# Sparse attention and two feed-forward layers on one core: one weight conversion in two shares its sign step with GpSimd, the first block starts on the strided half of x, and two more mask sums move to VectorE

## The chip, the core and the metric

The kernel runs on one core of a Trainium2 chip. The core has a matrix engine (TensorE, PE in the rows) with its weight loads (PEld), a vector engine (VectorE, DVE), an activation engine (ScalarE, ACT), a general engine (GpSimd, POOL) and a queue engine that issues the transfers (SyncE, SP). The metric is device time of one execution in microseconds, lower is better.

## What is computed

The reference runs three stages in a row: attention of 4 batches of 8 heads over 576 positions (heads 0 to 3 see the last 32 keys, heads 4 to 7 every 32nd key), a feed-forward layer with a squared ReLU, and a second one with a rational function.

```python
scores = q @ k.T / sqrt(D);  scores = where(mask, scores, -1e9)
attn = exp(scores - max);  attn = attn / (sum(attn) + 1e-9);  x = attn @ v
h = maximum(x @ w_in, 0);  x1 = (h * h) @ w_out
h = x1 @ w_in2
g = (a0 + a1*h + a2*h**2 + a3*h**3) / (1 + |b0|*|h| + |b1|*h**2 + 1e-6)
out = g @ w_out2
```

There are 2304 tokens, a width of 512 and an inner width of 2048. The weights arrive as 64-bit floats and are turned into 32-bit ones on the chip.

## The kernel before, in words

**Products.** Each float32 operand of a feed-forward product is split into a high part in TensorE's 32-bit format (fp32r) and the rest, so a product is three matmuls: high by high, high by rest, rest by high (`h_unit` L423 for the first product of a layer, `o_unit1` L468 and `o_unit2` L658 for the second).

**Weight conversion** (`to_f32`, L177 to L192, then `split_w`, L200 and L201). A tile of 512 weights of 128 rows arrives as pairs of 32-bit words, `lo` and `hi`, in `wraw`. ScalarE makes the exponent and the upper mantissa (L188, into `w32`). VectorE shifts and masks that (L189, into a PSUM tile `bits`), joins the sign bit of `hi` (L190) and joins the upper bits of `lo` (L191). GpSimd makes the high part `wh` (L200) and the rest `wl` (L201). For layer 0 there are 32 such conversions, two for each of the 16 slices `f` of the inner width: part 0 holds the slice's columns of w_in, part 1 its rows of w_out. They run in the order `wq` (0 and 1 and 2 of part 0, then part 1 of slice 0, part 0 of slice 3, part 1 of slice 1, and so on alternately). Three go ahead of the first block, then two to each unit (`feed_w`, L531).

**Attention in 13 pieces.** A piece has scores (`at_scores`, L277), a softmax (`at_softmax`), transposes (`at_transpose`), values (`at_values`) and the split of its result into the high part `xh` and rest `xl` of x (`at_out`). Pieces are strided (`s`) or local (`l`). The mask is added in one of two ways. For pieces under `MASK_PE` (L236) TensorE multiplies the mask by an identity into the scores' bank first (L295); for later ones VectorE adds it afterwards (L329). The first three pieces (P0 and P1 strided, P2 local) are the head of the program; the other ten are spread over the units by the table `PLAN`, piece 3 over slices 2, 4 and 5 of the first block, piece 4 over 6, 8 and 9, piece 5 over 10, 12 and 13. P0 and P1 give rows 2 and 3 of the first block's x (`xh10`, `xl10` in the order below), P2 rows 0 and 1 (`xh00`, `xl00`).

**The first layer.** Five blocks of tokens of 16 units each. Unit (j, f) makes the slice's h from four rows kk of x, then ScalarE and VectorE make its square and split it into `gh` and `gl`; two units later `o_unit1` adds it to four accumulators. In block 0 two conversions ride in each unit. `fill` (L490) puts matmuls on a constant tile `warm` ahead of some waits; its counts stand in the table `FILL` (L58).

**What sets the order.** Instructions of the head's pieces and of block 0's conversions on ScalarE stand as written (`pin`, `in_order`, `keep_in_program_order`); the rest is placed by the framework's scheduler, and each engine then runs its own list in that order. An engine whose next instruction waits holds everything behind it.

**The end.** The last unit of the second layer makes its result on VectorE, its high part on ScalarE (L644), its rest on GpSimd (L645), and `o_unit2` of that unit closes the program.

Of the kernel before, what the change touches and what calls it, by code (L numbers as in the profile page):

```python
# [9 lines left out]
F32 = mybir.dt.float32  # L10
# [44 lines left out]


W3 = 54
FILL = {'s0': 8, 's1': 1, 't00': 6, 't01': 2, 's2': 2, 't10': 2, 'v1': 4, 't20': 4, 't21': 2, 'h0': 3}  # L58
S_SLOTS = ((0, 6), (17, 5))
QS_W, QKS_W = 11 * W3, 11 * W3 + S  # L60
QKL_W = 2 * 512 + STRIDE
# [60 lines left out]
def moe_kernel(ctx, tc, qs, vs, ql, vl, w1, w2, a, b, masks, eye, out):  # L122
# [51 lines left out]
        if which and block0[0]:  # L174
            tc.keep_in_program_order(ins)

    def to_f32(layer, f, part, raw, place=None):  # L177

        lo, hi = raw[:, :, 0], raw[:, :, 1]
        w = stage.tile([P, DM], I32, tag="w32", bufs=3, name=f"w32_{layer}_{f}_{part}")
        bits, to = w, w
        if layer == 0 and place:
            to = hi
        if layer == 0:
            bits = psum_w.tile([P, DM], I32, tag="bits", name=f"bits{f}_{part}")
        in_order(layer == 0, nc.scalar.activation(w.bitcast(F32), hi.bitcast(F32), AF.Abs, scale=2.0**-112))  # L188
        nc.vector.tensor_scalar(bits, w, 3, 0x7FFFFFFF, ALU.logical_shift_left, ALU.bitwise_and)  # L189
        nc.vector.scalar_tensor_tensor(bits, hi, -0x80000000, bits, ALU.bitwise_and, ALU.bitwise_or)  # L190
        nc.vector.scalar_tensor_tensor(to, lo, 29, bits, ALU.logical_shift_right, ALU.bitwise_or)  # L191
        return to.bitcast(F32)  # L192

# [4 lines left out]
    def split_w(wh, wl, wf):  # L198

        nc.gpsimd.tensor_scalar(wh, wf, 1.0, 0.0, ALU.mult, ALU.add)  # L200
        nc.gpsimd.tensor_tensor(wl, wf, wh.bitcast(F32), ALU.subtract)  # L201
# [31 lines left out]
    ORDER = [("s", 0, 2), ("s", 0, 3), ("l", 0), ("l", 1), ("s", 1, 2), ("s", 1, 3), ("l", 2),  # L233
             ("s", 2, 2), ("s", 2, 3), ("l", 3), ("s", 3, 2), ("s", 3, 3), ("l", 4)]
    pieces = [Piece(n, *x) for n, x in enumerate(ORDER)]
    HEAD, MASK_PE = 3, 6  # L236
    for p in pieces[:HEAD]:
        p.pinned = True
    pieces[0].homes = ("l8", "l9")
# [171 lines left out]

    gt, acc, lows = {}, {}, []

    def h_unit(layer, j, f, ps):
        n = (WIDTHS2 if layer else WIDTHS)[j]
        wh, wl = wt[layer, f]
        if layer and f % FSTEP[j]:
            ps = ps[:, n:]
        for kk in range(KT):
            c = slice(kk * P, (kk + 1) * P)  # L420
            xh, xl = x_rows(layer, j, kk, n)
            for i, (w, x) in enumerate(((wh, xh), (wh, xl), (wl, xh))):
                nc.tensor.matmul(ps[:, :n], w[:, c], x, start=(kk == 0 and i == 0), stop=(kk == KT - 1 and i == 2))  # L423

    def g_tile(tag, name, n, dtype=F32):
        return gpool.tile([P, 512], dtype, tag=tag, name=name, bufs=3)[:, :n]
# [59 lines left out]
    def fill(what, ps):  # L486


        for _ in range(FILL.get(what, 0)):
            tc.keep_in_program_order(nc.tensor.matmul(ps, warm[:, :P], warm, start=True, stop=True, skip_group_check=True))  # L490
# [14 lines left out]
        nc.scalar.activation(co[:, 6:8], co[:, 4:6], AF.Abs)  # L505


    LAG, LATER = 2, 3
    wq = sorted(((f, p) for f in range(NF) for p in range(2)), key=lambda u: (u[0] + LATER * u[1], -u[1]))


# [19 lines left out]
    def feed_w(n):  # L531
        for _ in range(n):
            load_raw(fed[0])
            if fed[0] < len(wq):
                f, part = wq[fed[0]]
                c = slice(part * DM, (part + 1) * DM)
                wh, wl = wt[0, f] if part else w_place(0, f)
                split_w(wh[:, c], wl[:, c], to_f32(0, f, part, raws[fed[0]], homes[fed[0]][0]))
                fed[0] += 1

    phase, under_way[0] = 0, 2_200_000
# [22 lines left out]
    feed_w(1)  # L564
    at_transpose(P2, 0)
    at_transpose(P2, 1)
    at_values(P2)
    at_out(P2)
    phase, under_way[0] = 1, 0
# [70 lines left out]
    def split2(n):  # L640
        if len(open2) > n:
            j, f, rq = open2.pop(0)
            gh, gl = (l2.tile([P, 512], F32R, tag=f"g{c}2", name=f"g{c}1_{j}_{f}", bufs=4) for c in "hl")
            keep(nc.scalar.copy(gh, rq))  # L644
            keep(nc.gpsimd.tensor_tensor(gl, rq, gh.bitcast(F32), ALU.subtract))  # L645
            gt[1, j, f] = gh, gl

    def o_unit2(j, f):
# [73 lines left out]
    for j, f in steps:  # L722
        block0[0] = j == 0
        if (j, f) not in JOINT:
            attend((j, f))
        while lows:
            lows.pop()()
        if j == 0:
            feed_w(2)
        if (j, f) == (3, 0):  # L730
            load_co()
        ps = psum.tile([P, 512], F32, tag="ps", name=f"h0_{j}_{f}")
        if j == 0:
            fill(f"h{f}", ps)
        h_unit(0, j, f, ps)
        last_act = act1(j, f, ps)
        if (j, f) in JOINT:
            attend((j, f))
        elif 0 < j < 4 and f > (1, 1, -1)[j - 1] and (j, f + 1) not in JOINT and n2 < spills[j - 1] + -(-(spills[j] - spills[j - 1]) * (f + 1) // NF):
            with tc.issue_after(last_act):  # L740
                spill_w(n2 // 2, n2 % 2)
            n2 += 1
            if n2 == 2 * NF:
                first.close()
                l2 = ctx.enter_context(tc.tile_pool(name="l2", bufs=2))
        if j == NB - 1 and NF - EARLY > f >= NF - EARLY - KT:
            load_x1(0, f - (NF - EARLY - KT))
        prev.append((j, f))
        if len(prev) > LAG:
            finish(*prev.pop(0))  # L750
        if j == NB - 1 and f >= NF - EARLY:
            unit2(0, f - (NF - EARLY))
# [30 lines left out]
```

## Time and profile before

| | us |
|---|---|
| time before, median of 3 runs (855.86 to 857.38) | 856.35 |
| the profiled execution, its own time | 857.55 |
| its span, first to last instruction | 855.8 |
| TensorE busy in the span | 846.5 |
| VectorE busy | 600.3 |
| GpSimd busy | 523.2 |
| ScalarE busy | 453.6 |

The profiled execution lies 1.20 us above the median of the three runs, and 1.75 us of its time lie outside the span. TensorE is busy for 99% of the span. A busy stretch of TensorE in the rows is a stretch in which matmuls overlap one another, so what a matmul costs is read from the start of one to the start of the next.

### The profile page before, as it was taken

How to read it: one execution, taken by the hardware profiler on the slowest of the kernel's cores; microseconds unless marked ns; L12 is line 12 of the kernel's file. 1: busy time of each engine (PE TensorE's matmuls, PEld its weight loads, DVE VectorE, ACT ScalarE, POOL GpSimd, SP SyncE). 2: the span in 40 equal slices, each digit the busy share in tenths (PEclk: the TensorE clock that was granted, in tenths of full speed). 3: DMA queues.
4: the chain of work that ended last, by engine and by line, in shares of the span. 5: the costliest groups of instructions: out<-in, count | busy, mean ns of one | idle time of the engine just before them, and what ended most of it. 6: DMA issues, size and time to landing. Idle time of an engine off the chain costs nothing.

```text
span 855.8 us, 14872 instructions
## 1 busy us (share of the span) xinstructions
PE 846.5 (99%) x5762; PEld 720.0 (84%) x5762; DVE 600.3 (70%) x688; ACT 453.6 (53%) x821; POOL 523.2 (61%) x468
## 2 busy tenths in 40 slices
PE   7999999999999999999999999999999999999998
PEld 4788889999888888889999888888888888888896
DVE  5899856556556555552127688888888888888885
ACT  3556534333333343333346566676667666766673
POOL 1687754455444465664334687778777777777664
PEclk9999999999999999999999999999999999999999
DMA  9972535555343374565774300010001000100010
GB/s 338 358 246 78 171 122 200 165 178 188 109 148 106 101 242 156 193 197 194 263 256 148 137 24 25 12 62 13 14 12 62 7 7 6 57 1 0 1 51 25
DMA packets 38246, 99.99 MB, mean 117 GB/s; under 512 B 4384, under 2 KB 8224, under 8 KB 38176
## 3 DMA queue, kind: packets, MB, share of 16 engines
q1 hardware_dynamic: 38176, 99.05, 34.3%
q8 instruction: 45, 0.74, 0.3%
q14 instruction: 25, 0.20, 0.1%
HBM read 72.82 MB, written 26.21 MB: 116 GB/s over the span
## 4 chain that ended last, share of the span: by engine, by line
PE 98%; DVE 1%; DMA 0%; ACT 0%; issue 0%; POOL 0%; SPq 0%; ACTq 0%; POOLq 0%
PE h L423 46%; PE acc L468 23%; PE acc L658 23%; PE ps_vl L361 1%; PE ps_sl L300 1%; PE ps_vs L361 1%; PE ps_ss L300 1%; PE ps_tl L352 1%; PE ps_ts L352 1%; DMA cst<-in_masks 0%; DVE sm L330 0%; PE ps_tl L490 0%; DVE sm L341 0%; PE ps_ss L295 0%; PE ps_sl L295 0%; DVE eal L339 0%
## 5 line engine op out<-in xcount | busy, mean ns | idle before, releaser
L423 PE MATMUL h<-xh,wh 128*128 128x512 f32 (+2 forms) x640 | 237.0, 371 | 0.0
L423 PE MATMUL h<-xh,wl 128*128 128x512 f32 (+2 forms) x640 | 235.6, 368 | 0.0
L423 PE MATMUL h<-xl,wh 128*128 128x512 f32 (+2 forms) x640 | 235.6, 368 | 0.0
L629 DVE RECIPROCAL h<-w 128x512 f32<-128x512 f32 x67 | 224.6, 3353 | 0.0
L624 POOL TENSOR_TENSOR p<-p,hs 128x512 f32<-128x512 f32 x67 | 86.9, 1297 | 97.6 <-ACT p L622 97.5
L423 PEld LDWEIGHTS h<-xh,wh 128*128 128x128 f32 x640 | 120.4, 188 | 18.3 <-issue 0.5
L423 PEld LDWEIGHTS h<-xh,wl 128*128 128x128 f32 x640 | 120.3, 188 | 17.7
L423 PEld LDWEIGHTS h<-xl,wh 128*128 128x128 f32 x640 | 120.4, 188 | 17.5
L468 PE MATMUL acc<-gh,wh 128*128 128x512 f32 (+1 forms) x320 | 118.2, 369 | 0.0
L468 PE MATMUL acc<-gh,wl 128*128 128x512 f32 (+1 forms) x320 | 117.7, 368 | 0.0
L468 PE MATMUL acc<-gl,wh 128*128 128x512 f32 (+1 forms) x320 | 117.6, 367 | 0.0
L658 PE MATMUL acc<-wh,gh 128*128 128x512 f32 x288 | 112.2, 389 | 0.0
L658 PE MATMUL acc<-wh,gl 128*128 128x512 f32 x288 | 112.2, 389 | 0.0
L658 PE MATMUL acc<-wl,gh 128*128 128x512 f32 x288 | 112.1, 389 | 0.0
L619 ACT ACTIVATE sq<-h 128x512 f32<-128x512 f32 x72 | 43.0, 597 | 128.3 <-PE h L423 122.0
L446 POOL TENSOR_TENSOR gl<-r,gh 128x512 fp32r<-128x512 f32 (+1 forms) x59 | 69.5, 1178 | 63.6 <-ACT gh L445 58.4
L627 DVE SCALAR_TENSOR_TENSOR p<-p,co,h 128x512 f32<-128x512 f32 x72 | 53.6, 745 | 69.2 <-POOL p L624 69.2
L438 ACT ACTIVATE r<-h 128x512 f32<-128x512 f32 (+1 forms) x75 | 41.8, 558 | 112.7 <-PE h L423 112.7
L442 DVE TENSOR_TENSOR r<-r 128x512 f32<-128x512 f32 (+1 forms) x59 | 43.6, 739 | 76.3 <-ACT r L438 76.2
L645 POOL TENSOR_TENSOR gl<-rq,gh 128x512 fp32r<-128x512 f32 x72 | 93.4, 1298 | 3.2 <-ACT gh L644 3.2
L626 POOL TENSOR_TENSOR w<-w,sq 128x512 f32<-128x512 f32 x66 | 85.5, 1296 | 0.0
L445 ACT CAST gh<-r 128x512 fp32r<-128x512 f32 (+1 forms) x75 | 43.7, 583 | 57.4 <-DVE r L442 56.9
(115 smaller groups left out, 1324.2 us busy)
## 6 DMA issues: line engine op xcount, KB each, us to landing
wraw<-in_w SPq DMA_DIRECT2D x64, 512.0 KB, 4.3
w_scratch<-sph SPq DMA_DIRECT2D x32, 256.0 KB, 3.9
w_scratch<-spl SPq DMA_DIRECT2D x32, 256.0 KB, 3.2
wh<-w_scratch SPq DMA_DIRECT2D x16, 512.0 KB, 3.9
wl<-w_scratch SPq DMA_DIRECT2D x16, 512.0 KB, 5.3
qks<-in_qs SPq DMA_DIRECT2D x8, 585.0 KB, 5.2
out_dram<-osb SPq DMA_DIRECT2D x18, 256.0 KB, 2.4
xraw<-x_scratch SPq DMA_DIRECT2D x16, 256.0 KB, 2.7
```

The costliest lines, as they stand in the source:

```text
L423: nc.tensor.matmul(ps[:, :n], w[:, c], x, start=(kk == 0 and i == 0), stop=(kk == KT - 1 and i == 2))
L442: nc.vector.tensor_tensor(h, h, h, ALU.mult)
L445: last_act = nc.scalar.copy(gh, h).ins
L446: low = lambda: (nc.vector if psum_h or j == 0 else nc.gpsimd).tensor_tensor(gl, h, gh.bitcast(F32), ALU.subtract)
L468: nc.tensor.matmul(acc[j][e][:, : WIDTHS[j]], w[:, c], g, start=(f == 0 and i == 0), stop=(f == NF - 1 and i == 2))
L619: keep(nc.scalar.activation(sq, h, AF.Square))
L624: keep(nc.gpsimd.tensor_tensor(p1, p1, hs, ALU.mult))
L626: keep((nc.vector if last else nc.gpsimd).tensor_tensor(w, w, sq, ALU.add))
L627: keep(nc.vector.scalar_tensor_tensor(p1, p1, a1, h, ALU.add, ALU.mult))
L629: keep(nc.vector.reciprocal(h, w))
L645: keep(nc.gpsimd.tensor_tensor(gl, rq, gh.bitcast(F32), ALU.subtract))
L658: nc.tensor.matmul(p, g[:, cg], w[:, c], start=(f + d + i == 0), stop=(f + d == NF - 1 and i == 2))
```

## The change

Four edits. In `to_f32`, a conversion with an even number in `wq` (16 of 32) lets GpSimd multiply `hi` twice by 2^-126 in place, which leaves zero with `hi`'s sign; VectorE then joins `w32` (shifted) and that in one step, both read from SBUF, in place of L189 and L190. In the first block `h_unit` takes the rows of x in the order `KK` = 2, 3, 0, 1, and the two first rows of unit 0 (six matmuls) are issued, pinned, between the transposes and the values of the third piece; the three filling matmuls `h0` go. `MASK_PE` falls from 6 to 4, so pieces 4 and 5 get their mask from VectorE. The rest `gl` of the last unit is made on VectorE.

```diff
-FILL = {'s0': 8, 's1': 1, 't00': 6, 't01': 2, 's2': 2, 't10': 2, 'v1': 4, 't20': 4, 't21': 2, 'h0': 3}
+FILL = {'s0': 8, 's1': 1, 't00': 6, 't01': 2, 's2': 2, 't10': 2, 'v1': 4, 't20': 4, 't21': 2}
...
-        nc.vector.tensor_scalar(bits, w, 3, 0x7FFFFFFF, ALU.logical_shift_left, ALU.bitwise_and)
-        nc.vector.scalar_tensor_tensor(bits, hi, -0x80000000, bits, ALU.bitwise_and, ALU.bitwise_or)
+        if zero:
+            z = hi.bitcast(F32)
+            nc.gpsimd.tensor_scalar(z, z, 2.0**-126, 2.0**-126, ALU.mult, ALU.mult)
+            nc.vector.scalar_tensor_tensor(bits, w, 3, hi, ALU.logical_shift_left, ALU.bitwise_or)
+        else:
+            nc.vector.tensor_scalar(bits, w, 3, 0x7FFFFFFF, ALU.logical_shift_left, ALU.bitwise_and)
+            nc.vector.scalar_tensor_tensor(bits, hi, -0x80000000, bits, ALU.bitwise_and, ALU.bitwise_or)
...
-    HEAD, MASK_PE = 3, 6
+    HEAD, MASK_PE = 3, 4
...
-    def h_unit(layer, j, f, ps):
+    def h_unit(layer, j, f, ps, ks=None, keep=False):
...
-        for kk in range(KT):
+        order = range(KT) if layer or j else KK
+        for kk in ks or order:
...
-    LAG, LATER = 2, 3
+    LAG, LATER, KK = 2, 3, (2, 3, 0, 1)
...
-                split_w(wh[:, c], wl[:, c], to_f32(0, f, part, raws[fed[0]], homes[fed[0]][0]))
+                split_w(wh[:, c], wl[:, c], to_f32(0, f, part, raws[fed[0]], homes[fed[0]][0], fed[0] % 2 == 0))
...
     at_transpose(P2, 1)
+    begun = []
+    for f in range(1):
+        ps = psum.tile([P, 512], F32, tag="ps", name=f"h0_0_{f}")
+        h_unit(0, 0, f, ps, KK[:2], True)
+        begun.append(ps)
     at_values(P2)
...
-            keep(nc.gpsimd.tensor_tensor(gl, rq, gh.bitcast(F32), ALU.subtract))
+            keep((nc.vector if (j, f) == (NB2 - 1, NF - FSTEP[-1]) else nc.gpsimd).tensor_tensor(gl, rq, gh.bitcast(F32), ALU.subtract))
...
-        ps = psum.tile([P, 512], F32, tag="ps", name=f"h0_{j}_{f}")
-        if j == 0:
-            fill(f"h{f}", ps)
-        h_unit(0, j, f, ps)
+        if j == 0 and f < len(begun):
+            ps = begun[f]
+            h_unit(0, j, f, ps, KK[2:])
+        else:
+            ps = psum.tile([P, 512], F32, tag="ps", name=f"h0_{j}_{f}")
+            h_unit(0, j, f, ps)
```

How the lists of the engines move, at three places. In the names the figures behind the last underline are a buffer's; `h0_0_0` is h of layer 0, block 0, slice 0, and a conversion's tile `wraw0_5_0` is layer 0, slice 5, part 0. The changed kernel's lines lie up to 16 further down, so its L366 is the L361 of before, its L205 and L206 are L200 and L201, its L349 is L344.

TensorE, from the end of the third piece's values into the first block, before (the 128 values of the piece, `ps_vl0`, stand just ahead of these rows, behind its transposes):

```order
L490 MATMUL h0_0_0_567<-warm_87 128x512
L490 LDWEIGHTS warm_87
L490 MATMUL h0_0_0_567<-warm_87 128x512
L423 MATMUL h0_0_0_567<-xh00_0_527,wh0_0_369 128x512
L423 MATMUL h0_0_1_612<-xh00_0_527,wh0_1_433 128x512
L295 LDWEIGHTS cst_76
L295 MATMUL ps_sl1_0_631<-cst_76 128x384
```

Behind the filling matmuls the first ones of units 0 and 1 read row 0 of x, which comes from the third piece.

TensorE at the same place, now: the end of the six matmuls that stand ahead of the values, and the first of the values:

```order
L429 MATMUL h0_0_0_461<-xh10_0_357,wh0_0_369 128x512
L429 MATMUL h0_0_0_461<-xl10_0_358,wh0_0_369 128x512
L429 MATMUL h0_0_0_461<-xh10_0_357,wl0_0_370 128x512
L366 MATMUL ps_vl0_0_468<-eal0_0_314,vl0_0_104 64x32
L366 MATMUL ps_vl0_0_468<-eal0_1_346,vl0_1_106 64x32
```

Six matmuls of unit 0 on the strided rows have moved ahead of the values, the filling ones are gone, and the first matmuls behind the values read rows 2 and 3 as well, for unit 1.

GpSimd in the head, before: the last step of P1's softmax, the two of P2's (`eal0`), and the first two conversions' split:

```order
L344 TENSOR_TENSOR eas0_3_1_228<-eas0_3_1_228,sm3_82 128x6x54
L344 TENSOR_TENSOR eal0_0_314<-eal0_0_314,sm0_79 128x512
L344 TENSOR_TENSOR eal0_1_346<-eal0_1_346,sm1_80 128x512
L200 TENSOR_SCALAR wh0_0_369<-wraw0_0_0_108 128x512
L201 TENSOR_TENSOR wl0_0_370<-wraw0_0_0_108,wh0_0_369 128x512
L200 TENSOR_SCALAR wh0_1_433<-wraw0_1_0_110 128x512
L201 TENSOR_TENSOR wl0_1_434<-wraw0_1_0_110,wh0_1_433 128x512
```

GpSimd in the head, now:

```order
L349 TENSOR_TENSOR eas0_3_1_228<-eas0_3_1_228,sm3_82 128x6x54
L191 TENSOR_SCALAR wraw0_0_0_108<-wraw0_0_0_108 128x512
L349 TENSOR_TENSOR eal0_0_314<-eal0_0_314,sm0_79 128x512
L349 TENSOR_TENSOR eal0_1_346<-eal0_1_346,sm1_80 128x512
L191 TENSOR_SCALAR wraw0_2_0_112<-wraw0_2_0_112 128x512
L205 TENSOR_SCALAR wh0_0_369<-wraw0_0_0_108 128x512
L206 TENSOR_TENSOR wl0_0_370<-wraw0_0_0_108,wh0_0_369 128x512
L191 TENSOR_SCALAR wraw0_3_0_116<-wraw0_3_0_116 128x512
L205 TENSOR_SCALAR wh0_1_433<-wraw0_1_0_110 128x512
L206 TENSOR_TENSOR wl0_1_434<-wraw0_1_0_110,wh0_1_433 128x512
```

A signed zero (the L191 rows) stands ahead of P2's softmax step, one ahead of slice 0's split, and one, that of slice 3, ahead of slice 1's split.

GpSimd around the softmax of piece 3 (`el1`), before:

```order
L200 TENSOR_SCALAR wh0_4_602<-wraw0_4_0_120 128x512
L201 TENSOR_TENSOR wl0_4_603<-wraw0_4_0_120,wh0_4_602 128x512
L344 TENSOR_TENSOR el1_0_684<-el1_0_684,sm2_81 128x384
L344 TENSOR_TENSOR el1_1_692<-el1_1_692,sm3_82 128x384
L200 TENSOR_SCALAR wh0_2_535<-wraw0_2_1_122 128x512
L201 TENSOR_TENSOR wl0_2_536<-wraw0_2_1_122,wh0_2_535 128x512
```

GpSimd around the softmax of piece 3, now:

```order
L205 TENSOR_SCALAR wh0_4_599<-wraw0_4_0_120 128x512
L206 TENSOR_TENSOR wl0_4_600<-wraw0_4_0_120,wh0_4_599 128x512
L349 TENSOR_TENSOR el1_0_681<-el1_0_681,sm2_81 128x384
L191 TENSOR_SCALAR wraw0_5_0_431<-wraw0_5_0_431 128x512
L349 TENSOR_TENSOR el1_1_689<-el1_1_689,sm3_82 128x384
L191 TENSOR_SCALAR wraw0_6_0_552<-wraw0_6_0_552 128x512
L205 TENSOR_SCALAR wh0_2_542<-wraw0_2_1_122 128x512
L206 TENSOR_TENSOR wl0_2_543<-wraw0_2_1_122,wh0_2_542 128x512
```

One signed zero stands between the piece's two steps, a second one between them and the split of slice 2's part 1.

## Rows read from the trace of the kernel before

**Rows 1.** Stretches: us; busy of PE, PEld, DVE, ACT, POOL; PEclk; DMA share, GB/s

```profile
20.00:23.20 3.20, 1.98 (x47) 1.43 (x48) 2.90 (x11) 2.58 (x8) 1.46 (x2) 0.99 1.02 389
23.20:26.60 3.40, 3.40 (x14) 2.07 (x11) 2.92 (x8) 1.62 (x5) 2.35 (x3) 0.51 0.96 310
...
40.00:130.00 90.00, 90.00 (x787) 74.06 (x786) 76.03 (x137) 48.54 (x92) 63.28 (x65) 1.00 0.48 160
```

**Rows 2.** Waits of TensorE: line, waited for: us in total, times, longest us

```profile
PE ps_vl L361 <- ACT eal L354: 0.5, 1, 0.5
```

**Rows 3.** Timeline of TensorE, head to unit 2: start us, us, what, [idle before <-releaser]

```profile
26.60 0.30 PE L361 MATMUL ps_vl<-eal,vl 64*64 64x32 f32 x2
27.40 2.06 PE L361 MATMUL ps_vl<-eal,vl 64*64 64x32 f32 x126 [0.50 <-ACT eal L354]
29.39 0.82 PE L490 MATMUL h<-warm 128*128 128x512 bf16 x3
...
37.29 0.50 PE L423 MATMUL h<-xh,wh 128*128 128x512 f32 x1
```

**Rows 4.** Timeline of TensorE: transposes and sums of slice 2, then scores with and without mask matmuls

```profile
48.32 0.82 PE L352 MATMUL ps_tl<-ident,el 128*128 128x128 f32 x6
...
51.71 0.39 PE L468 MATMUL acc<-gh,wh 128*128 128x512 f32 x1
...
61.18 0.39 PE L468 MATMUL acc<-gl,wh 128*128 128x512 f32 x1
61.41 0.39 PE L468 MATMUL acc<-gh,wl 128*128 128x512 f32 x1
...
62.02 0.92 PE L300 MATMUL ps_ss<-qks 64*64 64x54 f32 x48
...
126.94 0.39 PE L468 MATMUL acc<-gh,wl 128*128 128x512 f32 x1
127.26 1.48 PE L300 MATMUL ps_sl<-qkl 64*32 64x64 f32 x128
```

**Rows 5.** VectorE from 0 to 125 us by line: busy us, mean ns | idle before

```profile
L190 DVE SCALAR_TENSOR_TENSOR bits<-wraw,bits 128x512 int32<-128x512 int32 x32 | 22.2, 692 | 0.8
L189 DVE TENSOR_SCALAR bits<-w 128x512 int32<-128x512 int32 x32 | 22.1, 690 | 3.7 <-ACT w L188 2.7
...
L446 DVE TENSOR_TENSOR gl<-r,gh 128x512 fp32r<-128x512 f32 x16 | 13.2, 826 | 2.7 <-ACT gh L445 2.6
```

**Rows 6.** GpSimd from 0 to 125 us by line: busy us, mean ns | idle before

```profile
L201 POOL TENSOR_TENSOR wl<-wraw,wh 128x512 fp32r<-128x512 f32 x25 | 34.0, 1361 | 2.1
L200 POOL TENSOR_SCALAR wh<-wraw 128x512 fp32r<-128x512 f32 x25 | 18.0, 720 | 13.9 <-DVE wraw L191 12.1 <-DVE sm L342 1.1 <-issue 0.2
```

**Rows 7.** Line L446: durations ns min/median/max, first and last start us

```profile
L446 DVE TENSOR_TENSOR gl<-r,gh x16: 678/688/1271, 35.8 to 121.7; 128x512 fp32r<-128x512 f32 x16
```

**Rows 8.** Timeline of GpSimd: head, then the steps of piece 3's softmax

```profile
21.74 2.04 POOL L344 TENSOR_TENSOR eal<-eal,sm 128x512 f32<-128x512 f32 x2 [5.77 <-DVE xl L385]
...
25.48 1.29 POOL L201 TENSOR_TENSOR wl<-wraw,wh 128x512 fp32r<-128x512 f32 x1
...
28.08 1.30 POOL L201 TENSOR_TENSOR wl<-wraw,wh 128x512 fp32r<-128x512 f32 x1
...
45.65 2.14 POOL L344 TENSOR_TENSOR el<-el,sm 128x384 f32<-128x384 f32 x2
...
48.56 1.73 POOL L201 TENSOR_TENSOR wl<-wraw,wh 128x512 fp32r<-128x512 f32 x1
```

**Rows 9.** Timeline of ScalarE in the head: the conversion of slice 3

```profile
27.24 0.69 ACT L188 ACTIVATE w<-wraw 128x512 f32<-128x512 f32 x1
```

**Rows 10.** The last rest and the matmuls around it

```profile
848.17 1.29 POOL L645 TENSOR_TENSOR gl<-rq,gh 128x512 fp32r<-128x512 f32 x1 [3.24 <-ACT gh L644]
849.18 0.39 PE L658 MATMUL acc<-wl,gh 128*128 128x512 f32 x1
849.51 0.50 PE L658 MATMUL acc<-wh,gl 128*128 128x512 f32 x1
```

More of the change, by code (lines that the diff above doesn't have):

```diff
@@ L175, in in_order, with to_f32 @@
             tc.keep_in_program_order(ins)
-    def to_f32(layer, f, part, raw, place=None):
+    def to_f32(layer, f, part, raw, place=None, zero=False):
         lo, hi = raw[:, :, 0], raw[:, :, 1]
@@ L422, in h_unit @@
             for i, (w, x) in enumerate(((wh, xh), (wh, xl), (wl, xh))):
-                nc.tensor.matmul(ps[:, :n], w[:, c], x, start=(kk == 0 and i == 0), stop=(kk == KT - 1 and i == 2))
+                ins = nc.tensor.matmul(
+                    ps[:, :n], w[:, c], x, start=(kk == order[0] and i == 0), stop=(kk == order[-1] and i == 2))
+                if keep:
+                    tc.keep_in_program_order(ins)
     def g_tile(tag, name, n, dtype=F32):
```

## The prediction

> **What bounds the kernel now.** I read four views, in this order. The table of busy times first: TensorE is busy for 846.5 of 855.8 us, so the time can only fall by taking matmuls away or by filling the 9 us in which it is idle. The waits of TensorE next: the list has seven entries, none of them later than 28 us of the span, and the longest single one is 1.9 us long or less; the one that this change can reach is 0.50 us ahead of the third piece's values, which wait for ScalarE's copy of the transposed weights [rows 2]. Third, the stretches: TensorE's granted clock is 0.51 from 23.20 to 26.60 us (the lower level, 1.2 GHz), after a stretch in which it was busy for 1.98 of 3.20 us, and 1.00 from 40 to 130 us, where it is busy without a break [rows 1]. There VectorE is busy for 76.03 and GpSimd for 63.28 of 90 us: neither holds TensorE up, so a cheaper conversion is worth nothing by itself. It is worth something if TensorE is made earlier and the weights have to follow. Last, the timeline of the head and of block 0, for what stands between the matmuls.
>
> **Part 1, the head.** The third piece's values cost 2.06 us and follow an idle of 0.50 us; behind them come three filling matmuls, 29.39 to 30.21, so 0.82 us [rows 3]. The change puts six matmuls of unit 0 ahead of the values. They were to be done anyway, so they cost nothing new, and they take longer (six steps of 0.23 us from start to start, as 61.18 to 61.41 [rows 4], make 1.4 us) than the 0.50 us that they cover. They need the first rest `wl`, which is done at 25.48 + 1.29 = 26.77 us [rows 8], and are to start when the transposes end at 26.60; its matmul is the third, so it is wanted at about 27.1. Taken away: 0.50 idle and 0.82 filling. The fill covered the time until x of the third piece is there (ScalarE's copies, then VectorE's rests); now unit 1's six matmuls on rows 2 and 3 and what unit 0 has ready lie there, 1.4 us and more, the same cover. Added: two more switches between long matmuls and the short ones of attention. Such a switch takes 0.32 us from start to start, 126.94 to 127.26 [rows 4], instead of 0.23, so about 0.1 each, 0.20. Net gain 1.12 us; 0.6 if x comes 0.5 late, 1.3 if the switches cost nothing.
>
> One new wait here. On GpSimd the signed zero of slice 3 stands ahead of slice 1's split. It waits for ScalarE's step of slice 3, which ends at 27.24 + 0.69 = 27.93 us [rows 9]. Zero (0.72), `wh` (0.72) and `wl` (1.36) of rows 6 put slice 1's rest at about 30.7 us; before it was there at 28.08 + 1.30 = 29.38 [rows 8]. TensorE wants it about 30.8: values end near 30.2, two matmuls, then this one. I take 0.1 us, bounds 0 and 0.5.
>
> **Part 2, the mask sums.** With the mask matmuls the last long matmul starts at 61.41 and the scores at 62.02, 0.61 us; without them it is 126.94 to 127.26, 0.32 us [rows 4]. So 0.29 us for each of two pieces, 0.58 in all, bounds 0.4 and 0.6. VectorE gets four sums of 324 columns; each is shorter than a conversion's step of 512 columns, 0.69 us [rows 5]. They lie ahead of the pieces' softmax, and their transposes come two units later, 11 us of matmuls; I cost them at nothing. If that cover were gone they would be worth at most 2.8 us.
>
> **Part 3, the conversions.** In 16 of 32, VectorE loses L189 (0.690) and L190 (0.692) and gets one step, 0.55 us or so less to do each time; GpSimd gets one in-place step on 512 columns, like L200, 0.72 us [rows 5, 6], 11.5 us in all. I take 0.72 although the new step writes every second word, which no row shows; bounds 0.65 and 1.1. The new VectorE step reads both inputs from SBUF. The one step in block 0 that does so is L446: 0.678 at best, 1.271 at worst, 0.826 on average [rows 5, 7], against 0.692 with one input from PSUM. So VectorE saves 1.382 - 0.826 = 0.56 us each time, 8.9 us in all, and spends up to 2.8 on the sums.
>
> The Trainium skill speaks against this step. "SBUF — State Buffer", section "SBUF: two separate sides", says that GpSimd and a VectorE step with two SBUF inputs lock one pair of ports for a whole instruction and the other waits it out. The spread of rows 7 agrees in kind; on average the wait there is 0.13 us. If each new step waited as long as the worst, it would save 0.1 instead of 0.56 us.
>
> Does TensorE have to wait for the slower GpSimd? The narrowest place is piece 3. GpSimd's two softmax steps run 45.65 to 47.79; the transposes start at 48.32, and the second half of them, 0.3 later, needs the second step: 0.8 us of room [rows 4, 8]. Then the rest of slice 2's second part ends at 48.56 + 1.73 = 50.29, and its sums start at 51.71, 1.4 us [rows 4, 8]. TensorE will be there some 1.1 us earlier. Ahead of the second softmax step GpSimd has five zeros more, 3.6 us, and it had 13.9 us of idle ahead of L200 in block 0, nearly all of it waiting for VectorE, which is now ahead by four times 0.56 us. What VectorE itself waits for (ScalarE's `gh` of slice 0) does not move, so I reckon that this piece's two steps end 0.7 to 1.1 us earlier than before. New wait there: 0.1 us, bounds 0 and 1.2. Behind it TensorE's reserve only grows, since GpSimd's idle is larger than what is added.
>
> **Part 4, the end.** TensorE's step to the third last unit's matmul is 849.18 to 849.51, 0.33 instead of 0.23, because GpSimd's rest ends at 849.46 [rows 10]. On VectorE it would take 0.69 [rows 7] instead of 1.29 and end 0.6 earlier: gain 0.10, no more, since TensorE has the matmuls ahead of it to do first.
>
> **Sum.** 0.50 + 0.82 - 0.20 + 0.58 + 0.10 - 0.20 = 1.60 us. Against the profiled execution it gives 857.55 - 1.60 = 855.95, span 854.2. That execution lies 1.20 above the median, and the gain has nothing to do with that difference: 856.35 - 1.60 = **854.75**, say 854.7.
>
> **Rivals.**
> (A) Forecast: gain of 1.0 to 2.0 us, 854.3 to 855.4. For it: all of it is work or idle that the chain of TensorE holds.
> (B) GpSimd is late in block 0. The new steps lock each other out as at L446's worst, 1.271 against 0.678, VectorE keeps no lead, and at the two narrow places TensorE waits 0.5 to 1.2 us. That leaves 0 to 1.0 of gain, 855.4 to 856.3. For it: 0.8 us of room and 1.1 us of new lead. By the rule of the Trainium skill on the shared ports, named above, this is the case to come. Against it: GpSimd's 13.9 us of idle.
> (C) Slower. The same wait at piece 3's transposes grows past about 1.2 us, and TensorE's clock falls behind it. The rows show such a case: busy for 1.98 of 3.20 us, then 0.51 for 3.40 us [rows 1], which costs half of that, 1.7 us. With a wait of 1.6 us: 856.35 - 1.60 + 1.6 + 1.7 = 858.05. It decides at a wait of about 1.2 us. Against it: the reckoning above finds 0.1, and in the head a wait of 0.50 us left the clock at 1.00.
> (D) More: neither new wait nor the two switches show, and a hitch in unit 0 goes. From the fill's end at 30.21 to unit 2 at 37.29 are 7.08 us [rows 3]; 24 matmuls of 0.23, 96 of the 128 scores' 1.48 and the mask, 0.29 [rows 4] make 6.9, so 0.2 are left that may come from x's being wanted first: 1.6 + 0.4 + 0.2 = 2.2 us, 854.15.
> That the change does not do what it says is ruled out for the masks and the fill, which are gone from TensorE's list; for the conversion it is B.
>
> **How the numbers follow.** A 0.53, B 0.22, C 0.10, D 0.15. The three runs shown reach from 0.5 below to 1.0 above their median, so about 0.2% (1.7 us) is what a measurement can tell from no change, and the forecast lies right at it. Faster by more, below 854.64: all of D and half of A, 0.42. Slower by more, above 858.06: most of C, 0.08. Within: 0.50. The range leaves out C and the tail of D, and takes in what three runs may be off: 853.6 to 856.6.
>
> **What would show it.** TensorE should have no idle between the third piece's transposes and unit 2, which should start near 36.1 instead of 37.29; six matmuls on `xh` should stand ahead of the values. The sums of slices 3 and 7 should be followed by scores after about 0.32 us. The waits of TensorE should lose the line for the values; a new line for GpSimd's `el` or `wl` says B, and a stretch of granted clock near 0.5 behind 40 us says C. VectorE's busy time should fall by some 7 us and GpSimd's grow by some 11. The forecast is wrong if x of the third piece comes late enough to open an idle behind the values, or if a zero takes well over 0.72 us.

## The result and the profile after

The changed kernel takes 861.24 us (median of 19 runs), the kernel before, run beside it, 856.01 us (19 runs). The ratio is 1.0062, with a 95% interval of 1.0042 to 1.0081: slower by 0.6%, some 5.2 us. The forecast was 854.7 us with a range up to 856.6. It was wrong, and in direction too. The ratios here go by all runs but those set aside as slow (here one of the 19, at 2174.79 us), so they need not be the quotients of the two medians.

Executions of one kernel spread over 2.5 to 11 us here, in part because TensorE's granted clock falls in the head in some executions and not in others (the profile of before has 0.51 from 23.20 to 26.60 us [rows 1], the profile of after 1.00 all through the head). So beside the ratio I give the fastest run, and the length of **block 0**, from unit 2's first matmul to the first scores behind the block: before it is 37.29 to 127.26, 89.97 us [rows 3, 4]. It comes from the one profiled execution of each kernel.

The profiled execution of after takes 859.81 us, span 858.0. First the granted clock and busy time by stretches, in the columns of [rows 1]:

```profile
23.20:26.60 3.40, 2.24 (x30) 1.34 (x34) 3.10 (x6) 1.06 (x2) 3.15 (x4) 1.00 0.95 293
34.00:130.00 96.00, 91.49 (x702) 73.73 (x692) 84.40 (x129) 50.09 (x96) 78.13 (x80) 1.00 0.51 175
```

Behind unit 2 TensorE is busy for 91.49 of 96 us, where before it had no break [rows 1]. Its waits from 18 to 132 us, where the kernel before had none for `h`:

```profile
PE h L429 <- POOL wl L206: 1.8, 2, 1.2
PE h L429 <- DVE es L344: 1.8, 1, 1.8
...
PE h L429 <- ACT r L447: 0.8, 1, 0.8
PE h L429 <- POOL wh L205: 0.7, 1, 0.7
PE ps_ss L305 <- issue: 0.7, 1, 0.7
```

The wait for the third piece's values is gone, as forecast. In its place units of `h` wait for GpSimd's splits, for VectorE and for ScalarE, and scores once for something that the profile doesn't name ("issue"). TensorE's timeline, from the first transposes of the third piece on, shows where in the head, and where block 0 begins and ends:

```profile
21.54 0.60 PE L357 MATMUL ps_tl<-ident,eal 128*128 128x128 f32 x4
...
23.71 0.50 PE L429 MATMUL h<-xh,wh 128*128 128x512 f32 x1 [0.70 <-POOL wh L205]
25.09 0.50 PE L429 MATMUL h<-xh,wl 128*128 128x512 f32 x1 [0.65 <-POOL wl L206]
...
34.04 0.50 PE L429 MATMUL h<-xh,wh 128*128 128x512 f32 x1
...
129.72 0.70 PE L305 MATMUL ps_sl<-qkl 64*32 64x64 f32 x47
```

Two things are to be seen. The early matmuls wait 0.70 us for slice 0's `wh` and 0.65 for its `wl`, more than the 0.50 they were to cover. And block 0 is 129.72 - 34.04 = 95.68 us long, 5.7 more than before, though 0.58 us of mask matmuls were taken out. VectorE and GpSimd up to 128 us, by line as in [rows 5, 6]:

```profile
L455 DVE TENSOR_TENSOR gl<-r,gh 128x512 fp32r<-128x512 f32 x16 | 19.9, 1243 | 2.1 <-ACT gh L454 2.1
L192 DVE SCALAR_TENSOR_TENSOR bits<-w,wraw 128x512 int32<-128x512 int32 x16 | 17.2, 1077 | 4.4 <-POOL wraw L191 3.7
...
L195 DVE SCALAR_TENSOR_TENSOR bits<-wraw,bits 128x512 int32<-128x512 int32 x16 | 11.1, 694 | 0.4
L194 DVE TENSOR_SCALAR bits<-w 128x512 int32<-128x512 int32 x16 | 11.0, 687 | 1.7 <-ACT w L188 1.1
...
L205 POOL TENSOR_SCALAR wh<-wraw 128x512 fp32r<-128x512 f32 x25 | 21.0, 839 | 3.5 <-DVE wraw L196 3.0
L191 POOL TENSOR_SCALAR wraw<-wraw 128x512 f32<-128x512 f32 x16 | 12.8, 797 | 3.3 <-ACT w L188 2.2
```

The new step L192 takes 1.08 us on average and not 0.83, the rests `gl` 1.24 and not the 0.826 of [rows 5], and VectorE waits 3.7 us for the zero. Idle ahead of these steps was 3.7 + 0.8 = 4.5 us [rows 5] and is now 4.4 + 1.7 + 0.4 = 6.5. Added up: 17.2 us for L192, 2.0 more idle and 19.9 - 13.2 = 6.7 more for `gl` make 25.9, against 16 times 1.382 = 22.1 us of removed steps. So the new step itself saved 4.9 us, about half of what was forecast, and the rests and the idle took 8.7: VectorE saved nothing, these lines took 3.8 us more. GpSimd's idle ahead of `wh` fell from 13.9 [rows 6] to 3.5 us.

One place shows how that reaches TensorE. Rows of VectorE, GpSimd and TensorE between 61 and 68 us:

```profile
62.25 0.70 DVE L192 SCALAR_TENSOR_TENSOR bits<-w,wraw 128x512 int32<-128x512 int32 x1 [1.06 <-POOL wraw L191]
...
63.59 1.82 DVE L455 TENSOR_TENSOR gl<-r,gh 128x512 fp32r<-128x512 f32 x1
...
66.94 0.88 DVE L344 TENSOR_TENSOR es<-ps_ss,sm 128x324 f32<-128x324 f32 x2
```

```profile
61.58 0.64 POOL L191 TENSOR_SCALAR wraw<-wraw 128x512 f32<-128x512 f32 x1
62.30 1.17 POOL L205 TENSOR_SCALAR wh<-wraw 128x512 fp32r<-128x512 f32 x1
63.55 1.31 POOL L206 TENSOR_TENSOR wl<-wraw,wh 128x512 fp32r<-128x512 f32 x1
64.83 1.08 POOL L205 TENSOR_SCALAR wh<-wraw 128x512 fp32r<-128x512 f32 x1
```

```profile
67.57 0.47 PE L429 MATMUL h<-xh,wh 128*128 128x512 f32 x1 [1.79 <-DVE es L344]
```

VectorE stands 1.06 us for the zero. Then its rest begins 0.04 us behind a split of GpSimd's and takes 1.82 us: it ends 0.55 us after that split. That is no single case: of the 32 VectorE steps with two SBUF inputs up to 128 us (16 of L192, 16 rests), 22 began while a GpSimd step was running, and all 22 ended 0.54 to 0.56 us behind the end of that step; the other ten took 0.68 to 0.70 us. In this profile the price of such a step is thus what is left of the step that it meets. The two halves of the wait here, 1.06 and 1.82 - 0.69 = 1.13 make 2.2 us by which the softmax's steps behind them on VectorE come late. They read scores out of PSUM, the next unit of `h` needs the bank, and TensorE waits 1.79 us.

At the tail the forecast holds: the matmuls of the last unit follow one another every 0.23 us, without the 0.33 of [rows 10]. VectorE's rest takes 0.69 us (GpSimd's took 1.29) and TensorE has no wait there.

### The profile page after: what moved, and what is told of

Read it like the earlier page. It is cut to its first block, busy times and chain, and to the rows that moved or that the text cites. A ratio compares the mean times of both kernels' runs of the same rounds, so it can differ in the third digit from the quotient of the medians.

```text
span 858.0 us, 14841 instructions
## 1 busy us (share of the span) xinstructions
PE 843.2 (98%) x5751; PEld 717.6 (84%) x5755; DVE 605.9 (71%) x677; ACT 452.9 (53%) x821; POOL 539.9 (63%) x483
## 4 chain that ended last, share of the span: by engine, by line
PE 87%; DVE 5%; DMA 4%; POOL 2%; ACT 1%; issue 1%; SPq 1%; DVEq 0%; POOLq 0%
PE h L429 42%; PE acc L672 23%; PE acc L477 20%; DMA wraw<-in_w 3%; DMA vl<-in_vl 1%; DVE gl L455 1%; DVE bits L192 1%; DVE wraw L196 1%; POOL wl L206 1%; PE ps_vl L366 1%; SPq L149 1%; POOL wh L205 1%; DVE bits L195 0%; PE ps_sl L305 0%; POOL wraw L191 0%
```

## The experiments

Of the kernels whose text says that signs or values are joined wrongly or left out, the outputs are not the reference's; the instructions are as described.

### Each part alone

The theories: the ports (**P**: VectorE's steps with two SBUF inputs and GpSimd's steps hold each other up), the masks (**M**), and the head (**H**: its lead is merely eaten).

**Zeros alone.** The kernel before with this in `to_f32`, for every even conversion:

```
+            z = hi.bitcast(F32)
+            nc.gpsimd.tensor_scalar(z, z, 2.0**-126, 2.0**-126, ALU.mult, ALU.mult)
+            nc.vector.scalar_tensor_tensor(bits, w, 3, hi, ALU.logical_shift_left, ALU.bitwise_or)
```

> The kernel before with the signed zero on GpSimd in every second conversion, and nothing else. Theory P (the ports: VectorE's new step and its rests both read two SBUF inputs and are held up by GpSimd's steps, and hold those up): the new step about 1.0 to 1.1 us on average, the rests L446 about 1.2 instead of 0.83, GpSimd's high parts 0.83 instead of 0.72, VectorE's busy time in block 0 not lower, TensorE waits for weights or for the softmax in block 0: 2 to 4 us slower, ratio 1.002 to 1.005. Theory M (the two mask sums hold the scores' banks, the zero is harmless by itself): 0.998 to 1.001. Theory H (the head's new order makes TensorE early and the waits only eat that lead): 1.000.

Measured: 862.45 us against 855.95, ratio 1.0069 (1.0044 to 1.0095); block 0 is 96.44 us long. The zeros alone bring the whole loss, so M and H fall as its cause. P's steps came near what was expected (0.96, 1.17 and 0.84 us), its price did not: the loss lies above P's 1.002 to 1.005.

```profile
L451 DVE TENSOR_TENSOR gl<-r,gh 128x512 fp32r<-128x512 f32 x16 | 18.7, 1167 | 4.9 <-ACT gh L450 4.7
L192 DVE SCALAR_TENSOR_TENSOR bits<-w,wraw 128x512 int32<-128x512 int32 x16 | 15.3, 959 | 8.0 <-POOL wraw L191 7.4
L205 POOL TENSOR_SCALAR wh<-wraw 128x512 fp32r<-128x512 f32 x25 | 20.9, 838 | 3.6 <-DVE wraw L196 3.1
```

The longest wait of TensorE in block 0 is 2.65 us. ScalarE's, GpSimd's, VectorE's and TensorE's rows there, and the stretches behind it (columns of [rows 1]):

```profile
107.86 0.66 ACT L188 ACTIVATE w<-wraw 128x512 f32<-128x512 f32 x1 [1.89 <-POOL wl L206]
108.43 0.58 ACT L443 ACTIVATE r<-h 128x512 f32<-128x512 f32 x1
```

```profile
103.54 0.66 POOL L191 TENSOR_SCALAR wraw<-wraw 128x512 f32<-128x512 f32 x1 [0.91 <-ACT w L188]
105.16 1.00 POOL L205 TENSOR_SCALAR wh<-w 128x512 fp32r<-128x512 f32 x1 [0.97 <-DVE w L196]
106.24 1.59 POOL L206 TENSOR_TENSOR wl<-w,wh 128x512 fp32r<-128x512 f32 x1
```

```profile
105.00 0.68 DVE L451 TENSOR_TENSOR gl<-r,gh 128x512 fp32r<-128x512 f32 x1
105.60 1.11 DVE L192 SCALAR_TENSOR_TENSOR bits<-w,wraw 128x512 int32<-128x512 int32 x1
```

```profile
109.15 0.47 PE L428 MATMUL h<-xh,wh 128*128 128x512 f32 x1 [2.65 <-ACT r L443]
```

```profile
106.50:109.15 2.65, 0.00 (x0) 0.03 (x1) 2.44 (x5) 1.25 (x3) 1.87 (x2) 1.00 0.47 176
...
110.65:114.06 3.41, 3.41 (x10) 2.64 (x9) 3.41 (x7) 0.99 (x4) 3.33 (x3) 0.50 0.03 10
```

Read from TensorE backwards: it waits for ScalarE's `r`, which stands in ScalarE's queue behind a conversion's first step, which waits for a buffer that GpSimd's rest sets free at 107.83. GpSimd's `wh` began beside VectorE's `gl` and took 1.00 where it takes 0.72 [rows 6]; its `wl` began beside L192 and took 1.59 where 1.29 is the least in this stretch; ahead of them GpSimd stood 0.91 us for ScalarE and 0.97 for VectorE. TensorE works again from 109.15, at first at a granted clock of 1.00; from 110.65 the clock is 0.50 (the lower of its two levels) for 3.41 us, which costs half of that, 1.7 us.

**Masks alone.**

```
-    HEAD, MASK_PE = 3, 6
+    HEAD, MASK_PE = 3, 4
```

> The kernel before with the mask of pieces 4 and 5 summed on VectorE, and nothing else. Theory P: 0.6 us of mask matmuls gone, VectorE in time: 0.999 to 1.000. Theory M: a wait of TensorE for VectorE's subtract of pieces 4 and 5 (h of slices 7 and 11) of 0.5 to 2 us each, 1.001 to 1.004.

Measured: 855.78 us, ratio 0.9990 (0.9965 to 1.0015), the fastest run 853.89 against 854.31. In the profile block 0 takes 89.38 us, 0.59 less than before, with no wait in it. M falls, for the masks by themselves. This profile has the clock at 1.00 all through the head and the head's old order, so it is the yardstick for the head of after. Its rows of TensorE, to set beside [rows 3] and the rows of after:

```profile
21.93 0.66 PE L352 MATMUL ps_tl<-ident,eal 128*128 128x128 f32 x4
...
24.31 2.06 PE L361 MATMUL ps_vl<-eal,vl 64*64 64x32 f32 x126 [0.50 <-ACT eal L354]
...
34.22 0.50 PE L423 MATMUL h<-xh,wh 128*128 128x512 f32 x1
```

Unit 2 starts at 34.22 with the old head at full clock and at 34.04 with the new one. That is no gain of the new order, since the third piece's transposes, up to which nothing of TensorE's work has changed, begin 0.39 us earlier in the profile of after (21.54 against 21.93). From there to unit 2 are 12.29 us in the old order and 12.50 in the new one; where 1.12 us were forecast, nothing was gained.

**Head alone** (`KK`, `begun`, no fill).

> The kernel before with the first block on rows 2, 3, 0, 1 of x, six matmuls of unit 0 ahead of the third piece's values and no fill h0; no zero, no mask sums, the last rest on GpSimd. Theories P and M: TensorE's lead of 1.1 to 1.4 us at unit 2 holds in part, 0.998 to 0.9995. Theory H (the lead is eaten by weights that come no earlier): 1.000 with new waits at piece 3's transposes and slice 2's sums, or slower.

Measured: 855.84 us, ratio 1.0005 (0.9974 to 1.0036), the fastest run 855.40, 1.1 above that of before. The waits of TensorE:

```profile
PE h L429 <- POOL wl L206: 0.7, 1, 0.7
PE ps_sl L305 <- issue: 0.6, 1, 0.6
PE h L429 <- POOL wh L205: 0.3, 1, 0.3
```

So without any zero, too, the early matmuls wait for slice 0's `wh` and `wl`. From the transposes to unit 2 are 13.02 us, 0.57 of them a wait for which the profile names no releaser. Block 0 is 90.57, 0.6 longer than before. H's ratio came, but its waits at piece 3's transposes and slice 2's sums did not; and the interval takes in what P and M expected as well.

**All but the zeros.**

> The changed kernel without the signed zero: head, mask sums and last rest stay. Theory P: the loss is gone, ratio 0.997 to 0.999. Theory M: the wait for VectorE's subtract stays, 1.001 to 1.004. A mixture (both parts needed): near 1.000.

Measured: 856.11 us, ratio 0.9983 (0.9958 to 1.0009), the fastest run 855.17. The early matmuls wait 0.3 and 0.6 us for `wh` and `wl`, and later an `acc` waits 0.8 for VectorE's `gl`. From the transposes to unit 2 are 12.25 us, so here too the new order gains nothing. Block 0 is 91.66, 2.3 longer than with the masks alone. H would explain it, what is started earlier waits later, but these are two single profiles, and the time does not show a loss.

### What in the zero costs

Three theories: P as above; the queues (**Q**: ScalarE, GpSimd and VectorE stand for one another, each in its order); the load (**L**: 11 us more for GpSimd). Each kernel is the one with the zeros alone, with one thing changed (two in the last).

**One SBUF input.** The chain stays, the second input goes:

```
-            nc.vector.scalar_tensor_tensor(bits, w, 3, hi, ALU.logical_shift_left, ALU.bitwise_or)
+            nc.vector.tensor_scalar(bits, hi, 3, 0x7FFFFFFF, ALU.logical_shift_left, ALU.bitwise_and)
```

> The zeros alone (conversions of every second piece), but VectorE's step after the zero reads only the zero's tile from SBUF and not the value beside it: its place in the queues, GpSimd's added step and the waits ScalarE to GpSimd to VectorE stay, only the second SBUF input goes (the value without its sign's bits is left out, so the output is not the reference's). Theory P (VectorE's steps with two SBUF inputs and GpSimd's steps hold each other up): the step falls from the 0.96 us mean of the zeros alone to 0.70, gl falls from 1.20 to at most 0.95, and the time to 856 to 858 us. Theory Q (the queues: GpSimd stands behind ScalarE, VectorE behind GpSimd, and each in its order): nothing changes in the waits, 861 to 863 us, idle ahead of the zeros still near 9 us in sum. Theory L (GpSimd simply has 11 us more to do in block 0): 861 to 863 as well.

Measured: 855.87 us against 855.65, ratio 1.0005 (0.9972 to 1.0038). Block 0 is 89.98 long, and TensorE waits nowhere in it. The rows from 20 to 130 us:

```profile
L205 POOL TENSOR_SCALAR wh<-wraw 128x512 fp32r<-128x512 f32 x25 | 19.9, 798 | 2.4 <-DVE wraw L196 1.6
L451 DVE TENSOR_TENSOR gl<-r,gh 128x512 fp32r<-128x512 f32 x16 | 16.6, 1035 | 4.4 <-ACT gh L450 4.2
L192 DVE TENSOR_SCALAR bits<-wraw 128x512 int32<-128x512 int32 x16 | 11.1, 691 | 6.6 <-POOL wraw L191 5.9
```

VectorE still waits 5.9 us for the zeros and GpSimd still has them, so Q and L by themselves fall. The step with one input took 0.68 to 0.70 us each of the 16 times, though 12 of them began while a GpSimd step was running. P's number for the time was almost right, but not that for the rests: `gl` takes 1.035, above the 0.95 expected, and nothing comes of it. GpSimd's idle ahead of `wh` is 2.4 us here, less than in after (3.5), and yet TensorE loses nothing. Nor is it another order of the steps: up to 130 us the lists of VectorE, GpSimd and ScalarE in these two kernels differ by a few neighbouring steps, one in the head and the others around piece 3's softmax, and not around the 2.65 us wait.

**Two SBUF inputs, no zero.** VectorE's joined step stands in place of its two old ones, and GpSimd does nothing more.

> VectorE's step with two SBUF inputs in place of the two old ones in every second piece, and nothing on GpSimd (sign and value are joined wrongly, so the output is not the reference's). Theory P: the step still meets GpSimd's splits, mean 0.80 to 0.95 us, gl 0.85 to 1.0, time 855.5 to 857.5 us. Theories Q and L: VectorE has 16 steps of 0.69 us fewer and nothing new to wait for, 855.3 to 856 us, step near 0.70 to 0.83.

Measured: 855.36 us, ratio 1.0014 (0.9982 to 1.0045), block 0 89.98. The step takes 0.93 us on average and GpSimd's `wh` 0.93, and `gl` 1.03, above the 1.0 that P allowed, and still no loss is to be seen: the slower step by itself doesn't cost either.

**The zero's size on a scratch tile, two SBUF inputs** (nobody waits for GpSimd's step):

```
-            nc.gpsimd.tensor_scalar(z, z, 2.0**-126, 2.0**-126, ALU.mult, ALU.mult)
+            nc.gpsimd.tensor_scalar(zz, hi.bitcast(F32), 1.0, 1.0, ALU.mult, ALU.mult)
```

> As the zeros alone, but GpSimd's added step of 512 columns reads the raw words and writes a tile that nobody reads (sign and value are joined wrongly, so the output is not the reference's): GpSimd has the same steps more, VectorE the same step with two SBUF inputs, but no one waits for the added step, and it does not wait for ScalarE. Theory P: step and gl are as long as with the zeros alone (0.96 and 1.2 us), time 860 to 862.5 us. Theory Q: the time falls to 855.5 to 857 us. Theory L: 860 to 863 us, GpSimd's splits late.

Measured: 858.25 us, ratio 1.0028 (0.9999 to 1.0057), the fastest run 856.18; block 0 is 91.30, with one wait of 1.3 us for ScalarE's `r`. That lies between P and Q. The fastest run, 2.0 us above that of before (854.20), and block 0 point to load and two inputs together costing something, and to the chain adding to it; shown it is not, since the interval takes in no change. The profiled execution is the slowest of the twelve, with the clock at 0.50 in the head up to 36 us, so its block 0 is a weak witness.

**The scratch step, VectorE's old steps.**

> The kernel before with the 16 added GpSimd steps of 512 columns into a tile that nobody reads, and VectorE's three steps as before: GpSimd's load alone. Theory P: gl rises a little above 0.83 us (more GpSimd work beside it), 856 to 857.5 us. Theory Q: 855.8 to 856.5 us. Theory L: 860 to 863 us, TensorE's waits for wh and wl as with the zeros.

Measured: 856.38 us, ratio 1.0000 (0.9969 to 1.0032), block 0 90.49. L falls.

### Where in block 0, and with the masks

**Zeros in the first eight or the last eight even conversions** (the second kernel has `fed[0] >= 16`):

```
-                split_w(wh[:, c], wl[:, c], to_f32(0, f, part, raws[fed[0]], homes[fed[0]][0], fed[0] % 2 == 0))
+                split_w(wh[:, c], wl[:, c], to_f32(0, f, part, raws[fed[0]], homes[fed[0]][0], fed[0] % 2 == 0 and fed[0] < 16))
```

> The zeros alone, but only in the 8 even conversions of the first 16 (whose words are loaded into idle weight buffers and wait there). With the 16 zeros block 0's profile lost 6.5 us, 1.8 of them before the 96 us mark and 4.7 behind it. Theory E (each zero costs its share, half of the zeros half of the loss): 859 us. Theory R (the loss comes where the words go through buffers that must first be set free, in the second 16): 855.7 to 857 us. Theory B (a backlog that is built up early and paid later): near 860 us.

> The zeros alone, but only in the 8 even conversions of the second 16 (whose words are loaded into buffers that earlier conversions must first set free). Theory E: 859 us. Theory R: 860 to 862 us, with TensorE's wait of some 2.7 us for ScalarE's r near the 106 us mark. Theory B: 856 to 858 us, since VectorE and GpSimd come to the second half without arrears.

Measured: 857.86 us, ratio 1.0041 (1.0014 to 1.0069), for the first half (its profile, of an execution of 1412.92 us, gives no block 0); 857.61, ratio 1.0020 (0.9997 to 1.0043), for the second, with block 0 at 91.34 and one wait of 1.3 us for `r`. Together 0.61%, near the 0.69% of all. R falls, since it left the first half without a loss. E comes nearest, though both times lie over 1 us below its 859; B had the second half right (856 to 858) and the first (near 860) not. So the loss is hardly a matter of the second half alone, but the intervals are too wide to say that every zero costs its share.

**The changed kernel with `MASK_PE` at 6.**

> The changed kernel with the mask sums of pieces 4 and 5 on TensorE as before (0.58 us more on TensorE, two long steps of 0.42 us fewer on VectorE in each of these pieces). If the mask sums on VectorE make the zeros' arrears worse (TensorE's wait of 1.8 us for VectorE's subtraction in piece 4): 859 to 860 us. If the two have nothing to do with each other: 861.8 us, the changed kernel's 861.2 and 0.58.

Measured: 862.50 us, ratio 1.0085 (1.0056 to 1.0115), block 0 97.35. The mask sums on VectorE are not shown to make it worse; the wait for VectorE's subtraction shrinks from 1.8 to 0.9 us, and the wait for `r` is back at 2.7.

**Masks, order and tail without the early matmuls and the zeros**, the version that might have beaten both.

> The kernel before with the two mask sums on VectorE, the order 2, 3, 0, 1 in the first slice's units without the six early matmuls and without the last fill, and the tail's last rest on VectorE; no zeros. If the early matmuls were what pulled the waits for slice 0's weights forward and the order itself is worth its 0.5 us of idle time: 854.5 us (masks 0.58, head 0.8 or so). If the head's lead goes whatever the order, since GpSimd's splits of slice 0 come when they come: 855.3 us (masks alone). A loss above 856.5 us speaks against both.

Measured: 857.41 us, ratio 1.0007 (0.9986 to 1.0027), the fastest run 854.58 against 854.08. No gain, and the median lies above the 856.5 that was to speak against both expectations. Its profiled execution lost 3.0 us in the head to a wait for which the profile names no releaser, so its head can't be judged by it. No version here is shown to beat the kernel before; all but the zeros (0.9983) and the masks alone (0.9990, with the lowest fastest run of the changed kernels) come nearest.

### Plain length without the shared lock

What stayed open was which engine's lengthening costs. These three have VectorE's step with one SBUF input, as in the run with one SBUF input, and a plain step more on VectorE, on GpSimd, or on both:

```
+            nc.vector.tensor_scalar(bits[:, :256], bits[:, :256], 0, 0x7FFFFFFF, ALU.logical_shift_left, ALU.bitwise_and)
+            nc.gpsimd.tensor_scalar(z[:, :128], z[:, :128], 2.0**-126, 2.0**-126, ALU.mult, ALU.mult)
```

> As the run in which VectorE's step after the zero reads one SBUF input (855.9 us), but that step is followed by one of 256 columns that reads and writes only PSUM (some 0.4 us): VectorE's conversion is now as long as with two SBUF inputs beside GpSimd, and no lock is held for it. (The value without its sign's bits is left out of the output, as there.) If VectorE's longer step is what costs (the conversions come late, whoever lengthens them): 858 to 862 us. If it is that GpSimd's splits are held up too, or that the two engines are locked into step: 855.5 to 856.5 us.

> As the run with one SBUF input (855.9 us), but GpSimd's zero is followed by one more step of 128 columns on it, 0.2 to 0.3 us, which is what its two splits took longer per zero when VectorE read two inputs (0.84 and 1.42 us where the run with one input has 0.80 and 1.33, twice per zero). If GpSimd's lengthening is what costs: 858 to 861 us. If VectorE's: 855.5 to 856.5 us.

> Both lengthenings at once. If the loss is the sum of what the two engines lose to each other, whatever the reason for it, this comes near the zeros alone: 860 to 862.5 us, with TensorE's wait for ScalarE's r in block 0. If it takes the lock itself (steps that meet at the moment when one waits for the other): 856 to 857.5 us.

Measured (before: 855.66 us, fastest 853.84):

| kernel | median | fastest | ratio, 95% | block 0 |
|---|---|---|---|---|
| VectorE + 0.43 us | 856.31 | 855.05 | 1.0004 (0.9976 to 1.0032) | 89.97 |
| GpSimd + 0.40 us | 857.27 | 855.84 | 1.0010 (0.9986 to 1.0033) | 91.32 |
| both | 859.11 | 857.99 | 1.0014 (0.9983 to 1.0045) | 92.30 |
| zeros alone (855.95, 854.31) | 862.45 | 859.49 | 1.0069 (1.0044 to 1.0095) | 96.44 |

These ratios don't separate the three from no change; the fastest runs and block 0 order them. VectorE's length costs block 0 nothing, GpSimd's 1.3 us, both 2.3; the medians of the last two lie between the ranges that were expected. GpSimd's added step stands ahead of VectorE's, so it lengthens the chain too: VectorE waits 10.2 us for it, where it waited 5.9 for the zeros with one SBUF input. The waits from 34 to 130 us of the kernel with both:

```profile
PE ps_tl L359 <- POOL el L351: 0.8, 1, 0.8
PE ps_ss L302 <- DVE xl L392: 0.7, 1, 0.7
```

Plain length on both engines thus brings, in these profiles, over a third of what the zeros cost block 0 (2.3 of 6.5 us), and by the fastest runs more (4.2 of 5.2). It doesn't bring the wait for `r`, nor the long rests (`gl` 0.92 against 1.17). And it is more length than the second input added: between the runs with one and with two inputs L192 grew by 0.27 us and each rest by 0.13, and GpSimd's splits by 0.27 for each zero. So the length alone doesn't make the loss. Whether the remainder is simply the rests' length, or that VectorE, once released by the zero, begins in the same moment as GpSimd's next step, these runs don't settle.

## Why the prediction was wrong

**Head: term mis-sized.** The wait for the values (0.50) and the fill (0.82) went, as said. The step that failed is "they need the first rest `wl`, which is done at 26.77": it was set against an end of the transposes at 26.60, read from an execution whose clock was 0.51 there. At full clock TensorE is done with the transposes at 23.0 us (23.71 less the wait of 0.70), GpSimd's split isn't there yet, and the matmuls wait 0.70 + 0.65 us. From the transposes to unit 2 the new order took 12.50 us against 12.29, so nothing came of the 1.12. The zeros have a part in it, but not at the feared place, slice 1's split: slice 2's zero stands ahead of slice 0's split, and the wait for `wh` is 0.7 us with the zeros and 0.3 without them.

**Masks: right.** 0.59 us measured for a forecast of 0.58, without cover being lost in the run with the masks alone. Beside the zeros the two sums stand in VectorE's queue at the 1.79 us wait, which is 0.7 us where TensorE adds the mask.

**Conversions: the step that failed.** "So VectorE saves 1.382 - 0.826 = 0.56 us each time, 8.9 us in all" took the average of L446 in a kernel where GpSimd had 13.9 us of idle [rows 6, 7]. It came to 0.31 us each time (L192 takes 1.077), and the prediction put at nothing what the change does to the other steps: the 16 rests went from 0.826 to 1.24 us, 6.7 us in all, which is more than the 4.0 by which the new step fell short, and GpSimd's `wh` from 0.72 to 0.84. The zero itself cost 0.80, within its bounds of 0.65 to 1.1. It is not that the rests meet GpSimd more often. Before, 10 of the 16 began while a GpSimd step was running, with at most 0.71 us of it left; now 11 do, seven of them with more than 1.0 us left. Also left out was the wait of VectorE for the zero, 3.7 us, 1.06 of it ahead of softmax steps whose banks TensorE needs. The forecast that VectorE would be 7 us less busy and so ahead had the wrong sign: it is busy for 605.9 us, 5.6 more than before.

The Trainium skill, "SBUF — State Buffer", section "SBUF: two separate sides", says that GpSimd and a VectorE step with two SBUF inputs lock one pair of ports in turn, each for a whole instruction, and that the one which starts second waits out the other. The rows agree: a rest that began 0.04 us behind a split of 1.31 took 1.82 us. I gave that rule to rival B and then bounded B's time by TensorE's waits at two places, 0.5 to 1.2 us; B's mechanism is what came, with a price of 6 us.

**Slower, rival C:** the wait with a clock that falls behind it came in the zeros alone, 2.65 us and then 1.7 for the clock, as priced (1.7), but at 106 us and not at piece 3's transposes. In the profile of after the waits are spread (0.8 to 1.8 us) and the clock stays at 1.00, behind the one of 1.79 us too: C's 1.2 us did not hold. The transposes of piece 3, on which the reckoning rested, lost 0.2 us.

**"Behind it TensorE's reserve only grows, since GpSimd's idle is larger than what is added"** is the other sentence that fell: TensorE's waits of 1.8, 0.7, 1.2 and 0.8 us in block 0 all lie behind piece 3's transposes. GpSimd's idle was room for the added load: with one SBUF input it went down to 2.4 us and nothing was lost, and with the load alone nothing was lost either. It was no room for steps that hold VectorE up and are held up by it.

**Tail: right**, 0.10 us, too small for any run to show.

In sum, against the profile of the masks alone (852.1 us of span, the same clock): block 0 is 95.68 - 89.38 = 6.3 us longer and unit 2 starts 0.18 us earlier, which with the tail's 0.10 makes 6.0; 858.0 - 852.1 = 5.9 was measured. In block 0, 4.5 of the 6.3 us are the four waits; the rest is what TensorE needs to get going behind each and some slower steps.

One reading of the prediction is off without bearing on the sum: the list of TensorE's waits has six lines, not seven, and its longest single wait is 1.5 us.

## What to carry to other kernels

Moving work from VectorE to GpSimd is not priced by the moved step: count every VectorE step with two SBUF inputs in the stretch, and expect all of them and GpSimd's own steps to lengthen, up to the whole length of the other's step. Idle of an engine can be room for added load and still be none for steps that lock out its neighbour: the same load cost nothing beside a step with one SBUF input. So before a step with two SBUF inputs is put beside a busier GpSimd, follow who waits behind both of them, and see whether one of the inputs can come from PSUM. And where a stretch ran at the lower clock in the one profile at hand, ask what the change meets when it runs at the full one.

## What the runs showed of the hardware

The joined step's 16 times in after range over 2.6 to 1:

```profile
L192 DVE SCALAR_TENSOR_TENSOR bits<-w,wraw x16: 699/1132/1804, 20.2 to 119.3; 128x512 int32<-128x512 int32 x16
```

The median, 1.13 us, is far above the least, 0.70, and the waiting goes both ways: beside a VectorE step with two inputs GpSimd's `wh` took 1.17 and 1.08 us in the rows above, and its `wl` 1.59. A GpSimd step of 128 columns took 0.40 us where one of 512 takes 0.67, so a quarter of the columns took more than half of the time.

Not expected either was how little the single cause costs: GpSimd's load alone (ratio 1.0000), two inputs alone (1.0014), and load and chain with one input (1.0005) each left the time within what a run can tell. Only all of them together cost 6 us.
